# Attention of a decode block in row form: running max with rescaled sums, V in 32 KB rows, c and x as one row

## The chip, the cores and the metric

The kernel runs on one core of a Trainium2 chip. The metric is the device time of one execution in microseconds (us). The runs of the kernel before lie between 439.77 and 440.72 us in all sets (0.2%). A ratio is the mean time of one kernel's fast runs over that of the other's of the same rounds, so it is not quite the ratio of the medians that are quoted.

A note on names: PE is the matmul engine, PEld its weight loads, DVE the vector engine, ACT the scalar engine, POOL the general one, SP the engine that issues the big loads. A packet is the piece of a load that one of the 16 DMA engines moves at a time, here one row of it. All times in the text are on the clock of the profile's views, with 0 at the first instruction; where the recorded texts give the time of a packet, it stands some 0.36 us later than on this clock.

## The reference

One token, one block: a conditioning vector gives six modulation rows, then grouped attention over a cache of 65,536 keys, then a gated feed-forward. Cut to what matters:

```python
# x [1,1,1024]; k_cache, v_cache [1,4,65536,128]; wq [1024,4096]; wo [4096,1024]
mod = silu(c) @ w_mod                       # [1, 6*1024]: sa, ca, ga, sb, cb, gb
h = layernorm(x) * (1 + ca) + sa
q = (h @ wq).reshape(32 heads, 128)         # 8 heads share one K/V head
p = softmax(q @ k.T * 128 ** -0.5)          # over 65,536 keys
x = x + ga * ((p @ v) @ wo)
h = layernorm(x) * (1 + cb) + sb
x = x + gb * ((gelu(h @ w_gate) * (h @ w_up)) @ w_down)
```

Everything is bfloat16. K and V are 64 MB each (67.1 million bytes) and all loads together 185.6 MB, so each byte is used once: a kernel of this kind streams.

## The kernel before

The big loads stand in one list. SP issues them in the order of the list, and each waits until the buffers that it overwrites are free ("released"). Attention runs over 32 chunks of 8,192 keys (2 MB of K, 2 MB of V). A step of PE works on three chunks at once: T (64 transposes of K, 128x128 each) of chunk i, QK of chunk i-1, PV of chunk i-2.

```python
head = iter([8, 0, 2, 4, 6, 8])                         # ten slots of 16 KB a partition
j_mod = [... plan_load(wmod_v[:, k:k + 2, :], ..., next(head), nslot=2) ...]   # 4 loads
j_q   = [... plan_load(wq_v[:, k:k + 4, :], ..., next(head), nslot=2) ...]     # 2 loads
blank = {}                                              # stands for the PV of chunks -2 and -1
for j in (-2, -1):
    blank[j] = Job(None, None, SITES + j % SITES)       # SITES = 4: slots 6 and 7
...
for i in range(NC + 2):                                 # NC = 32 chunks
    if i == SITES:
        j_o = [plan_o(k) for k in range(0, 16, 16)]     # half of wo into slots 8 and 9
    if i < NC and i % KU == 0:                          # KU = 2: K of two chunks, 32 KB rows
        j_k[i] = plan_load(kv_src(kh, i, KU), ..., i % SITES, kfill[...], KU)
    if i >= 2:
        j = i - 2                                       # V of one chunk, 16 KB rows
        j_v[j] = plan_load(kv_src(vh, j), ..., SITES + j % SITES, vfill[j % SITES])
# ... cut: the other half of wo, w_gate, w_up, w_down

def issue_ready():                                      # SP, in the order of the list
    while issued[0] < len(loads):
        j = loads[issued[0]]
        if any(q.freed is None for q in j.prev):
            return
        SP.wait(*(q.freed for q in j.prev))
        sp.dma_start(j.view, j.src).then_inc(j.tok[0], 16)
        issued[0] += 1

# one step of PE; the same instructions serve every four chunks in a hardware loop, so the
# first pass also runs QK of chunk -1 and PV of chunks -2, -1 on whatever is there
def QK(b):          # 64 of these a chunk: K^T (128x128) is the weight, q (8 columns) moves
    pe.matmul(sc_ps[:, base + n * REP:base + (n + 1) * REP], kt_sb[:, j % 2, n, :],
              q_buf[:, j % SITES, :], start=True, stop=True)
def PV(q):          # 64 of these: V (128x128) is the weight, P (8 columns) moves
    pe.matmul(b7[:, s * REP:(s + 1) * REP], j_v[j].view[:, n, :], p_sb[:, s, n, :],
              start=(n == 0), stop=(n == CH - 1))
T(0); QK(0); T(1); QK(1); PV(0); T(2); QK(2); QK(3); PV(1); T(3); PV(2); MT(); PV(3); MB()

for h in range(REP):                                    # ACT: eight exps a chunk
    act.activation(p_sb[:, s, :, h], scv[:, h, :], ACT.Exp, bias=mneg[:, j, h:h + 1],
                   scale=scale, accum_out=z_all[:, j, h:h + 1])
```

Each chunk has its own maximum. After the last chunk all partial sums are rescaled at once.

## Time and profile before

| | before |
|---|---|
| median of the runs | 439.9 us at first, 440.06 us with the runs beside the changed kernel |
| span in the profile | 438.6 us |
| share of the load queue | 98.8% of 16 DMA engines' span |
| PE, DVE, ACT busy | 345.6, 171.9, 146.4 us |
| summed packet time | 434.5 us per DMA engine |

The summary page of the kernel before, cut to the lines used. The span stands first, then the busy time of the engines, then the 40 equal slices of the span (each digit is the busy share in tenths, 9 is 90% or more, and GB/s is what the DMA engines moved), then the load queue with packets, megabytes and its share of 16 engines.

```profile
span 438.6 us, 15324 instructions
...
PE 345.6 (79%) x7107; PEld 315.0 (72%) x7107; DVE 171.9 (39%) x300; ACT 146.4 (33%) x553; POOL 11.7 (3%) x25
...
DMA  8999999999999999999999999999999999999995
GB/s 343 411 442 429 428 432 426 430 432 427 429 435 429 448 420 456 410 445 439 410 451 409 452 409 451 418 433 442 424 434 427 433 430 433 438 434 425 423 424 238
...
q1 hardware_dynamic: 9904, 185.60, 98.8%
...
slots<-in_A_k_cache_dram SPq DMA_DIRECT2D x16, 4096.0 KB, 20.9
slots<-in_A_v_cache_dram SPq DMA_DIRECT2D x32, 2048.0 KB, 26.9
```

The DMA row shows no pause between its first and last slice. PE at 79% looks like a rival. The loads do wait for the buffers that PE frees, but so much is queued meanwhile that the DMA engines do not run dry: a K load needs 9.7 us for its own 4 MB (at 432 GB/s, which is 16 engines with packets of 32 KB at 1214.4 ns each) and lands a median of 20.9 us after its issue, so other loads stand before it.

The second view is the timeline of SP of the kernel before, first lines: start, duration, and the load that was issued. It tells when each load may first move.

```profile
26.19 2.05 SPq L234 DMA_DIRECT2D slots<-in_A_k_cache_dram  x2
36.43 0.80 SPq L234 DMA_DIRECT2D slots<-in_A_v_cache_dram  x2
57.15 0.33 SPq L234 DMA_DIRECT2D slots<-in_A_wo_dram  x1
80.61 0.33 SPq L234 DMA_DIRECT2D slots<-in_A_k_cache_dram  x1
```

The first two V loads go out at 36 us, half of wo at 57 us. When PE begins its first step at 63 us, some 12 MB stand in the queue (K of two more chunks, the first two V loads, half of wo), which is 29 us of transfer. The third view is the chain of waits that ended last, in the stretch where attention begins (start, duration, what):

```profile
26.19 36.92 DMA slots<-in_A_k_cache_dram
63.24 1.89 PE kt_ps L562 x16
65.53 1.73 PE kt_ps L562 x16
```

The first K load lands, and PE's transposes follow.

### The profile page before, as it was taken

What the parts mean: (1) busy time and instruction counts of PE and PEld (TensorE: products, weight loads), DVE (VectorE), ACT (ScalarE), POOL (GpSimd) and SP (SyncE); (2) the same over time, 40 slices, a digit from 0 to 9 for tenths busy, and PEclk for the clock granted to TensorE, in tenths of its full rate; (3) what the DMA queues carried; (4) which work ended last, traced back from release to release, by engine and by line L of the source; (5) the groups of instructions that cost most, each with busy time, mean ns of one, the idle gap of its engine ahead of it and who ended that gap; (6) DMA issues with size and microseconds to landing.
All of it is one profiled execution on the core that took longest, in us unless ns stands there. A gap on an engine that the chain in (4) does not pass through costs nothing.

```text
span 438.6 us, 15324 instructions
## 1 busy us (share of the span) xinstructions
PE 345.6 (79%) x7107; PEld 315.0 (72%) x7107; DVE 171.9 (39%) x300; ACT 146.4 (33%) x553; POOL 11.7 (3%) x25
## 2 busy tenths in 40 slices
PE   0154669997989979998999889999799989547564
PEld 0022348897979979998999779998789989533234
DVE  0101015363644553564445544644445545142100
ACT  1000001434435644343446434345625434600000
POOL 8100000000000000000000000000000000000000
PEclk9995658696977895895579965959858886658955
DMA  8999999999999999999999999999999999999995
GB/s 343 411 442 429 428 432 426 430 432 427 429 435 429 448 420 456 410 445 439 410 451 409 452 409 451 418 433 442 424 434 427 433 430 433 438 434 425 423 424 238
DMA packets 10228, 185.88 MB, mean 424 GB/s; under 512 B 1376, under 2 KB 1376, under 8 KB 1760
## 3 DMA queue, kind: packets, MB, share of 16 engines
q1 hardware_dynamic: 9904, 185.60, 98.8%
q8 instruction: 13, 0.21, 0.2%
q10 hardware_dynamic: 304, 0.01, 0.0%
q14 instruction: 7, 0.06, 0.0%
HBM read 185.60 MB, written 0.00 MB: 423 GB/s over the span
## 4 chain that ended last, share of the span: by engine, by line
DMA 57%; PE 37%; DVE 2%; issue 2%; ACT 1%; SPq 1%; ACTq 0%; POOL 0%
DMA slots<-in_A_v_cache_dram 39%; PE kt_ps L562 18%; DMA slots<-in_A_k_cache_dram 8%; PE b L626 7%; DMA slots<-in_B_w_down_dram 6%; PE sc_ps L582 6%; DMA x_row<-in_A_x_dram 4%; PE kt_ps L393 3%; PE b L606 1%; PE b L373 1%; ACT p_sb L692 1%; PE b L596 1%; SPq L234 1%; DVE kt_sb L752 0%; PE sc_ps L454 0%
## 5 line engine op out<-in xcount | busy, mean ns | idle before, releaser
L562 PE MATMUL kt_ps<-ident,slots 128*128 128x128 bf16 x2048 | 176.7, 256 | 10.2 <-DMA slots<-in_A_k_cache_dram 9.5
L562 PEld LDWEIGHTS kt_ps<-ident,slots 128*128 128x128 bf16 x2048 | 152.6, 117 | 12.0 <-issue 6.6
L661 DVE COPY kt_sb<-kt_ps 128x2048 bf16<-128x2048 bf16 x96 | 117.5, 1224 | 108.9 <-PE kt_ps L562 108.8
L661 ACT ACTIVATE kt_sb<-kt_ps 128x2048 bf16<-128x2048 bf16 x32 | 60.1, 1877 | 178.4 <-PE kt_ps L562 178.4
L626 PE MATMUL b<-p_sb,slots 128*128 128x8 bf16 x2176 | 75.0, 167 | 23.6 <-DMA slots<-in_A_v_cache_dram 11.2
L626 PEld LDWEIGHTS b<-p_sb,slots 128*128 128x128 bf16 x2176 | 68.8, 99 | 26.2 <-issue 12.8
L692 ACT ACTIVATE p_sb<-sc_ps,mneg 128x64 bf16<-128x64 f32 x256 | 83.5, 561 | 7.2 <-DVE mneg L687 7.2
L692 ACT ACTIVATION_READ_ACCUMULATOR p_sb<-sc_ps,mneg 128x1 f32 x256 | 77.1, 366 | 0.0
L582 PE MATMUL sc_ps<-q_buf,kt_sb 128*128 128x8 bf16 x2112 | 69.8, 167 | 1.0 <-issue 1.0
L582 PEld LDWEIGHTS sc_ps<-q_buf,kt_sb 128*128 128x128 bf16 x2112 | 67.8, 100 | 1.1 <-issue 1.1
L393 PE MATMUL kt_ps<-slots,h_pad 128*32 128x512 bf16 x176 | 17.8, 547 | 15.4 <-DMA slots<-in_A_wq_dram 8.3
L393 PEld LDWEIGHTS kt_ps<-slots,h_pad 128*32 128x32 bf16 x176 | 6.1, 124 | 24.8 <-issue 11.2
L680 DVE TENSOR_REDUCE m_col<-sc_ps 128x8 f32<-128x512 f32 x32 | 21.8, 680 | 4.4 <-PE sc_ps L582 4.4
L685 DVE TENSOR_REDUCE mg<-b 8x1 f32<-8x128 f32 x32 | 8.9, 279 | 32.8 <-PE b L596 32.8
L464 PE MATMUL b<-ident,x_row 8*128 8x8 bf16 x1 | 0.2, 161 | 20.2 <-DMA x_row<-in_A_x_dram 20.2
L606 PE MATMUL b<-negi,mg 8*128 8x8 f32 x66 | 14.9, 296 | 0.0
L393 PE MATMUL kt_ps<-slots,s_pad 128*32 128x512 bf16 x96 | 10.7, 516 | 4.9 <-DMA slots<-in_w_mod_dram 4.9
L464 PEld LDWEIGHTS b<-ident,x_row 8*128 8x128 bf16 x1 | 0.1, 97 | 20.1 <-issue 20.1
L687 DVE COPY mneg<-b 128x8 f32<-128x8 f32 x32 | 5.3, 166 | 21.1 <-PE b L606 21.1
L454 PEld LDWEIGHTS sc_ps<-identf,kt_sb 128*128 128x128 f32 (+1 forms) x48 | 7.6, 204 | 8.2 <-DVE kt_sb L775 4.3
L606 PEld LDWEIGHTS b<-negi,mg 8*128 8x128 f32 x66 | 11.9, 223 | 2.2
L454 PE MATMUL sc_ps<-identf,kt_sb 128*128 128x128 f32 (+1 forms) x48 | 9.1, 352 | 4.5 <-DVE kt_sb L775 2.4
(97 smaller groups left out, 89.2 us busy)
## 6 DMA issues: line engine op xcount, KB each, us to landing
slots<-in_A_k_cache_dram SPq DMA_DIRECT2D x16, 4096.0 KB, 20.9
slots<-in_A_v_cache_dram SPq DMA_DIRECT2D x32, 2048.0 KB, 26.9
slots<-in_w_mod_dram SPq DMA_DIRECT2D x4, 3072.0 KB, 20.4
slots<-in_A_wq_dram SPq DMA_DIRECT2D x2, 4096.0 KB, 35.0
slots<-in_A_wo_dram SPq DMA_DIRECT2D x2, 4096.0 KB, 32.5
slots<-in_B_w_gate_dram SPq DMA_DIRECT2D x2, 3584.0 KB, 23.7
slots<-in_B_w_up_dram SPq DMA_DIRECT2D x2, 3584.0 KB, 22.9
slots<-in_B_w_down_dram SPq DMA_DIRECT2D x3, 2048.0 KB, 26.2
```

The costliest lines, as they stand in the source:

```text
L234: sp.dma_start(j.view, j.src).then_inc(j.tok[0], 16)
L393: ins = pe.matmul(out, pad[:, k, :], jb.view[:, kk, c0:c0 + ROW], start=k <= last_k[0], stop=k >= last_k[1], skip_group_check=True,)
L454: ins = pe.transpose(dst[:, i * w:i * w + n], src[:, a], identf[0:src.shape[0], 0:n])
L562: ins = pe.transpose(kt_ps[:, half * 2048 + t * P:half * 2048 + (t + 1) * P], j_k[i - i % KU].view[:, i % KU * CH + b * TB + t, :], ident[ ...
L582: ins = pe.matmul(sc_ps[:, base + n * REP:base + (n + 1) * REP], kt_sb[:, j % 2, n, :], q_buf[:, j % SITES, :], start=True, stop=True,)
L606: ins = pe.matmul(b6[:, 256:256 + REP], mg8[:, j % 2:j % 2 + 1].to_broadcast([REP, P]), negi[:, :], start=True, stop=True,)
L626: ins = pe.matmul(b7[:, s * REP:(s + 1) * REP], j_v[j].view[:, n, :], p_sb[:, s, n, :], start=(n == 0), stop=(n == CH - 1),)
L661: ev[i % SITES][b].done(act.activation(dst, src, ACT.Copy) if E_ is AC else dve.tensor_copy(dst, src))
L680: m1[s].done(dve.tensor_reduce(m_col[:, j % 2, :].unsqueeze(2), scv, AX.X, ALU.max))
L685: m2[s].done(dve.tensor_reduce(mg8[:, j % 2:j % 2 + 1], b6[0:REP, 32:32 + P], AX.X, ALU.max))
L687: v_mc[j] = DVE.done(dve.tensor_copy(mneg[:, j, :], b6[:, 256:256 + REP]))
L692: ins = act.activation(p_sb[:, s, :, h], scv[:, h, :], ACT.Exp, bias=mneg[:, j, h:h + 1], scale=scale, accum_out=z_all[:, j, h:h + 1],)
```

## The change

The intent: PE, busy for 79% of the span, should do the attention with fewer, wider matmuls, ACT should do one wide exp in place of eight narrow ones, V should come in larger pieces, and the small loads of c and x should not be 128 tiny rows. q and P become the stationary operands, in four column tiles of 32, and K^T and V move by 512 columns. P has then to be transposed (PT), which puts PV one step later (LAG = 3). The maximum runs on from chunk to chunk, and DVE rescales the sum of each chunk. The core of the diff, with the epilogue and the constants cut:

```diff
-        act.dma_start(c_in[:, :], c[0].rearrange("(p k) -> p k", p=P)).then_inc(c_sem, 16)
-        act.dma_start(x_in[:, :], A_x[0, 0].rearrange("(p k) -> p k", p=P)).then_inc(x_sem, 16)
-        act.dma_start(x_row[:, :], A_x[0, 0].rearrange("(j p) -> j p", p=P)).then_inc(in_sem, 16)
+        act.dma_start(c_row, c).then_inc(c_sem, 16)
+        act.dma_start(x_row, A_x[0]).then_inc(x_sem, 16)
@@ the list of loads
-        for j in (-2, -1):
-            blank[j] = Job(None, None, SITES + j % SITES)
+        for j in (-2 * VU, -VU):                      # VU = 2
+            blank[j] = Job(None, None, vslot(j))      # slots 4, 5 and slots 6, 7
+            blank[j].freed = None
-        for i in range(NC + 2):
+        for i in range(0, NC + KU, KU):
             if i == SITES:
-                j_o = [plan_o(k) for k in range(0, 16, 16)]
+                j_o.append(plan_o(0, 8))              # a quarter of wo into slot 8
-            if i < NC and i % KU == 0:
+            if i < NC:
                 j_k[i] = plan_load(kv_src(kh, i, KU), flat(KU * CH, DH), i % SITES, ...)
-            if i >= 2:
-                j = i - 2
-                j_v[j] = plan_load(kv_src(vh, j), flat(CH, DH), SITES + j % SITES, ...)
+            else:
+                j_o.append(plan_o(8, 9))
+            if i >= KU:
+                j = i - KU
+                j_v[j] = plan_load(kv_src(vh, j, VU), flat(VU * CH, DH), vslot(j), ..., VU)
@@ QK, per quarter chunk
-                    for t in range(TB):               # 16 of 8 columns
-                        pe.matmul(sc_ps[...], kt_sb[:, j % 2, n, :], q_buf[:, j % SITES, :], ...)
+                    for g in range(NQ):               # 4 of 512 columns, in 4 column tiles
+                        pe.matmul(sc(j)[QD * g:QD * (g + 1), :], q_buf[:, j % SITES, QD * b:QD * (b + 1)],
+                                  kt_sb[:, j % 2, n:n + w, :]..., start=b == 0, stop=b == NB - 1)
@@ PV
-                j = i - 2
+                j = i - LAG
-                        pe.matmul(b7[:, s * REP:(s + 1) * REP], j_v[j].view[:, n, :], p_sb[:, s, n, :], ...)
+                            pe.matmul(b7[QD * c:QD * (c + 1), :]..., p_sb[:, s, c * P + QD * g:...],
+                                      v[:, NQ * g + c, :, :], start=g == 0, stop=g == NQ - 1)
@@ ACT
-                for h in range(REP):
-                    act.activation(p_sb[:, s, :, h], scv[:, h, :], ACT.Exp, ...)
+                act.activation(al[:, j:j + 1], mneg[:, j - 1:j], ACT.Exp, ...)     # the rescale
+                act.activation(p_row[:, j % 2, :], sc(j), ACT.Exp, ..., accum_out=zr[:, j:j + 1])
@@ DVE, per chunk
-                    dve.tensor_copy(o_all[:, j, :], b7[...])
+                    dve.scalar_tensor_tensor(o_acc[:, :], o_acc[:, :], al[:, j:j + 1], b7[:, :], ALU.mult, ALU.add)
```

With LAG = 3 the first pass of the loop runs PV for chunks -3, -2 and -1, and chunk -3 reads slot 5. The first V load (slots 4 and 5) may therefore go out only after PV of PE's first step has run.

## The prediction

> **What bounds the kernel now.** The DMA. The summary page's queue table gives the load queue 98.8% of 16 engines' span, and the slices show 9 (90% or more) between the first and last, 424 GB/s on average. The packet records run from 2 us to 436 us of the 438.6 us span and sum to 434.5 us per engine (no hole). [...] the 32 KB packets here (1214 ns each, 16 engines) make 432[...]. PE is 79% busy, but in the chain of waits its pieces lie between K and V landings: a K load lands a median of 20.9 us after its issue, of which its own 4 MB take about 9.7, so some 11 us of other loads are queued before it.
>
> **What the change does.**
> 1. V in 32 KB instead of 16 KB packets. Mean packet times are 612.7 and 1214.4 ns: 11.1 ns saved per pair, 128 pairs per engine: -1.4 us, fully on the path.
> 2. wo goes from 32 to 16 KB: 16 pairs per engine, +0.2 us.
> 3. c and x as rows: 256 packets of 16 B go (0.14 us per engine), and 16 V completions (0.14 us): -0.3 us. The w_mod matvec starts sooner than 20.8 us, off the path: some 38 us of loads are queued then.
> 4. PE in attention: QK and PV go from 128 matmuls with 128x128 weights (34 to 39 ns each) to 32 of 512 columns in four column tiles (0.107 us each at half clock): about 5 to 3.5 us per chunk. The 64 transposes stay. ACT's eight exps with accumulator reads (2.6 us per chunk) become one wide exp, a rescale and a copy. All off the path: the DMA needs 9.7 us per chunk.
> 5. The softmax end (386.2 to 393 us) becomes a few small matmuls, off the path.
> 6. A new risk: the first V load now waits for the first PE step after K lands (63.2 us), not for w_mod (issued at 36.4 us). That step reaches the end of PV at about 69.5 us (estimated from that step's transposes, 1.9 us per 16), data 1.4 us later, about 71; the loads before it end at 71 to 73 us. I put 0 to 1 us of starved DMA on the path. Later V loads still find about 10 us queued.
>
> **Sum.** 439.9 - 1.4 + 0.2 - 0.3 + 0.4 = 438.8 us. Range 437.4 to 440.4. Chances: faster by over 2% 0.01, within 2% 0.97, slower 0.02.
>
> **What would show each step.** V packets averaging 1214 ns; a summed packet time of about 433 us per engine and a load queue still near 99%. PE busy falling, with its idle time now before K and V landings; ACT busy falling by more than a third. A slice below 9 near 70 us would be the starved start. The chain of waits should still end in w_down's landing and about 3 us after it.
>
> **What would make it wrong.** A larger hole at the first V load; V slots freed in pairs and late, so that the queue runs dry at each pair (GB/s in the slices then falls below 420 throughout); [...] the max chain stretching a chunk beyond 9.7 us; a packet rate that depends on which tensors are in flight.

## The result, and the profile after

| | before | after |
|---|---|---|
| median of 6 runs | 440.06 us (439.77 to 440.30) | 441.28 us (439.90 to 441.69) |
| ratio | | 1.0024, 95% interval 1.0010 to 1.0037 |
| span in the profile | 438.6 us | 439.5 us |
| summed packet time per DMA engine | 434.5 us | 433.0 us |
| mean packet of the load queue, of 16 KB and of 32 KB | 611.7 and 1214.4 ns | 612.0 and 1216.0 ns |
| packets of V | 4096 of 16 KB | 2048 of 32 KB |
| PE, DVE, ACT busy | 345.6, 171.9, 146.4 us | 315.2, 217.3, 111.2 us |

The class was right (within 2%), the sign was not: 438.8 us with a range up to 440.4 was stated, 441.28 us was measured. The same lines of the page, of the changed kernel:

```profile
span 439.5 us, 8993 instructions
...
PE 315.2 (72%) x4077; PEld 208.2 (47%) x4077; DVE 217.3 (49%) x403; ACT 111.2 (25%) x164; POOL 15.7 (4%) x20
...
DMA  8999998999999999999999999999999999999995
GB/s 356 432 441 435 429 428 347 425 429 429 429 429 432 436 435 433 441 435 435 429 429 432 429 432 429 430 435 435 435 441 435 432 415 438 428 436 435 421 420 229
...
q1 hardware_dynamic: 7888, 185.60, 98.3%
...
slots<-in_A_k_cache_dram SPq DMA_DIRECT2D x16, 4096.0 KB, 23.1
slots<-in_A_v_cache_dram SPq DMA_DIRECT2D x16, 4096.0 KB, 23.7
```

PE has 30 us less to do and nothing comes of it, as was expected. The packets cost 1.4 us less in sum over all queues, and 1.1 us less in the load queue (432.2 against 433.3 us per engine). But the seventh slice (65.9 to 76.9 us) moved 347 GB/s, against 426 before; that is the only 8 inside the DMA row. The slice is 11 us long, so its missing fifth is about 2 us.

The timeline of SP of the changed kernel, the same loads:

```profile
26.64 2.05 SPq L236 DMA_DIRECT2D slots<-in_A_k_cache_dram  x2
71.17 0.33 SPq L236 DMA_DIRECT2D slots<-in_A_v_cache_dram  x1
71.54 0.43 SPq L236 DMA_DIRECT2D slots<-in_A_wo_dram  x1
80.92 0.33 SPq L236 DMA_DIRECT2D slots<-in_A_k_cache_dram  x1
```

The first V load goes out at 71.17 us and its bytes move from 72.1 us on, 1.0 us later. Since wo stands after it in the list, wo waits with it, although its slot is free (in a run below, where wo stands earlier, it goes out at 56.17 us). What was issued earlier had drained, but not on all engines at once: in the packet records 16 engines are at work until 70.2 us, four from 70.5 to 71.2 us, one at 72.0 us, and 16 again at 72.9 us. Between 68 and 86 us an engine was idle for 1.7 us on average, against 0.1 us in the kernel before. The chain of waits in this stretch:

```profile
26.64 35.78 DMA slots<-in_A_k_cache_dram
62.42 3.60 issue
66.02 1.88 PE kt_ps L597 x16
68.45 1.49 PE kt_ps L597 x16
```

Here is what the chain of the kernel before did not have: K has landed at 62.42 us and PE begins at 66.02 us. "issue" means that PE waited for nothing that the profile shows.

A second measure is needed to say how much a gap costs. Take the bytes that each kernel has moved by a given moment, from the packet records, and express the lead of one over the other in us at 432 GB/s:

| moment, us | 20 | 60 | 68 | 80 | 150 | 250 | 350 | 420 |
|---|---|---|---|---|---|---|---|---|
| lead of after over before, us | +0.54 | +0.58 | +0.58 | -1.66 | -1.27 | -1.06 | -0.83 | -0.71 |

So the changed kernel wins 0.5 us in its first 20 us, loses 2.2 us between 68 and 80 us, and wins back 0.95 us over all of the attention. Its last load packet ends 1.0 us later than before's (436.4 against 435.4 us), and the times of the two profiled runs differ by as much (440.85 against 439.92 us).

### The profile page after: what moved, and what is told of

Read it like the earlier page. It is cut to its first block, busy times and chain, and to the rows that moved or that the text cites. A ratio compares the mean times of both kernels' runs of the same rounds, so it can differ in the third digit from the quotient of the medians.

```text
span 439.5 us, 8993 instructions
## 1 busy us (share of the span) xinstructions
PE 315.2 (72%) x4077; PEld 208.2 (47%) x4077; DVE 217.3 (49%) x403; ACT 111.2 (25%) x164; POOL 15.7 (4%) x20
## 4 chain that ended last, share of the span: by engine, by line
DMA 54%; PE 32%; DVE 11%; issue 2%; ACT 1%; POOL 0%; DVEq 0%; POOLq 0%
DMA slots<-in_A_k_cache_dram 42%; PE kt_ps L597 15%; DMA slots<-in_B_w_down_dram 8%; PE b L680 5%; PE sc_ps L619 4%; DMA slots<-in_A_v_cache_dram 4%; PE kt_ps L420 3%; DVE selt L353 3%; DVE kt_sb L719 2%; DVE s_pad L759 1%; DVE o_red L742 1%; PE b L646 1%; PE sc_ps L661 1%; DVE o_acc L732 1%; PE b L400 1%
## 5 line engine op out<-in xcount | busy, mean ns | idle before, releaser
L597 PE MATMUL kt_ps<-ident,slots 128*128 128x128 bf16 x2048 | 154.6, 236 | 36.4 <-DMA slots<-in_A_k_cache_dram 27.7
L597 PEld LDWEIGHTS kt_ps<-ident,slots 128*128 128x128 bf16 x2048 | 132.3, 106 | 62.4 <-issue 42.8
L777 ACT ACTIVATE p_sb<-sc_ps 128x512 bf16<-128x512 bf16 x32 | 19.1, 597 | 179.1 <-PE sc_ps L661 179.1
L619 PE MATMUL sc_ps<-kt_sb,q_buf 128*32 128x512 bf16 x528 | 52.1, 429 | 0.0
L680 PE MATMUL b<-slots,p_sb 128*32 128x512 bf16 x560 | 42.0, 426 | 3.2 <-DMA slots<-in_A_v_cache_dram 2.5
L732 DVE SCALAR_TENSOR_TENSOR o_acc<-o_acc,s_pad,b 128x512 f32<-128x512 f32 x28 | 20.9, 748 | 12.1 <-PE b L680 12.1
L680 PEld LDWEIGHTS b<-slots,p_sb 128*32 128x32 bf16 x560 | 16.3, 109 | 19.8 <-issue 8.6
L783 ACT ACTIVATE p_row<-sc_ps,s_pad 128x512 bf16<-128x512 f32 x32 | 21.7, 677 | 0.0
L759 DVE TENSOR_REDUCE s_pad<-sc_ps 128x1 f32<-128x512 f32 x28 | 19.1, 680 | 0.0
L646 PE MATMUL b<-mg,selt 8*128 8x1 f32 x66 | 12.7, 259 | 8.2 <-DVE mg L769 8.2
L646 PEld LDWEIGHTS b<-mg,selt 8*128 8x128 f32 x66 | 9.8, 186 | 11.8 <-DVE mg L769 11.7
L463 POOL TENSOR_TENSOR rs<-va,halfneg 128x1 f32<-128x1 f32 x2 | 1.1, 554 | 379.8 <-DVE va L460 379.8
```

Of the source, the lines that this page charges most:

```text
L597: ins = pe.transpose(kt_ps[:, half * 2048 + t * P:half * 2048 + (t + 1) * P], j_k[i - i % KU].view[:, i % KU * CH + b * TB + t, :], ident[ ...
L619: ins = pe.matmul(sc(j)[QD * g:QD * (g + 1), :], q_buf[:, j % SITES, QD * b:QD * (b + 1)], kt_sb[:, j % 2, n:n + w, :].rearrange("p n d -> ...
L646: ins = pe.matmul(b6[:, 256:257], selt[:, :], mg[:, j % 2:j % 2 + 1], start=True, stop=True,)
L680: ins = pe.matmul(b7[QD * c:QD * (c + 1), :].rearrange("p (b d) -> p b d", b=NB), p_sb[:, s, c * P + QD * g:c * P + QD * (g + 1)], v[:, NQ ...
L732: v = oc[j % SITES].done(dve.scalar_tensor_tensor(o_acc[:, :], o_acc[:, :], al[:, j:j + 1], b7[:, :], ALU.mult, ALU.add))
L759: v = DVE.done(dve.tensor_reduce(m_new, sc(j), AX.X, ALU.max))
```

## The experiments

Two theories. **H (the hole):** all of the loss is the one gap at 70 us, made by the order of the load list and the first PE step; the rest of the change is a small gain. **S (steady state):** V slots freed in pairs and a step late, or the new PE step, cost time all along. From the chain came a third question, **F**: why PE began 3.6 us after K had landed. The instruction queue's packet records ("q8 instruction" of the page, 10 packets of 16 KB in the changed kernel) show a packet of 16 KB at 63.42 us, 0.95 us long, and no other start in that queue between 29.8 and 69.1 us. F is the author's reading of that packet, to be tested: what PE runs after the wait for K came in this packet (a "block" in the texts below), and it was fetched only once that wait had passed.

All kernels below gave correct results. The kernel before ran beside them at 440.04 us in both sets. In four of them (wo_first, late, wo_first_late, before_v32) the runs fall into two groups 2 to 3 us apart, whose granted clocks do not differ, and in the first three the profiled run lies in the upper group. What parts the groups is open.

### wo_first: w_o ahead of the first V load

Edit, on the changed kernel:

```diff
-            if i == SITES:
-                j_o.append(plan_o(0, 8))
             if i < NC:
                 j_k[i] = plan_load(...)
-            else:
-                j_o.append(plan_o(8, 9))
+            if i == KU:
+                j_o += [plan_o(0, 8), plan_o(8, 9)]
             if i >= KU:
                 j_v[i - KU] = plan_load(...)
```

> The changed kernel with one edit: the two w_o loads into slots 8 and 9 (4 MB together, about 9.7 us of transfer) stand before the first V load in the load queue instead of after it and at the end. Theory H (hole): after lost 2.2 us at 70 to 76 us because the first V load waits for PE's first step; with 9.7 us of other bytes queued the gap closes, no 2 us stretch between 66 and 80 us falls below 90% of the mean rate, and the time is 441.3 - 2.2 = 439.1 us (438.3 to 439.7), below the kernel before (440.06). Rival S (steady state: V slots freed in pairs and a step late, or PE's new step, cost the time all along): the gap at 70 us may close but the time stays within 0.5 us of 441.3.

Measured: 439.27 us (six runs, five from 438.99 to 439.53, one of 441.57), ratio to before 0.9979 (0.9966 to 0.9992). The timeline of SP:

```profile
56.17 0.80 SPq L236 DMA_DIRECT2D slots<-in_A_wo_dram  x2
71.17 0.33 SPq L236 DMA_DIRECT2D slots<-in_A_v_cache_dram  x1
```

V still goes out at 71.17 us, but the lead over before stays at +0.5 us from 68 to 80 us: the gap is closed, and 2.0 us of the time go with it. S is out as the main cause, since PE and the V slots are as they were.

The profiled run was the one of 441.57 us, and it shows a gap of its own. The stretches of 360 to 370 us of this kernel (length, busy time of PE, PEld, DVE, ACT and POOL with counts, granted clock, DMA share, GB/s; a packet counts where it started, so that a share can pass 1):

```profile
360.00:365.00 5.00, 4.33 (x68) 3.42 (x64) 3.33 (x8) 2.71 (x4) 0.00 (x0) 1.00 0.95 341
365.00:370.00 5.00, 5.00 (x82) 3.35 (x81) 4.64 (x6) 1.08 (x3) 0.00 (x0) 1.00 0.97 413
```

The edit had also taken the second w_o load away from its place before the last V pair, so that the queue ran thin there: the lead over before falls by 1.25 us between 360 and 380 us. The other five runs are 2 us faster; whether they had this gap is not known.

### late, and wo_first_late: the loop held back, without and with w_o first

Edit of both, on the changed kernel and on wo_first:

```diff
+        GP.wait(v_q)
+        GP.wait(GP.done(pool.memset(kt_sb[:, 1, 0:48, :], 0.0)))
+        v_late = GP.done(pool.memset(kt_sb[:, 1, 16:64, :], 0.0))
-        PE.wait(t1, v_const, v_q, v_zero)
+        PE.wait(t1, v_const, v_q, v_zero, v_late)
```

> The changed kernel with PE's loop held back: two clears of an unused tile on POOL (about 5.2 us each) after q is ready, which PE waits for, so that PE's first step starts at 69.4 us (or at 72.8 if the 3.6 us stall seen before it is repeated) instead of 66.0. Theory H: the first V load goes out that much later and every us is lost: time up by the shift of PE's first instruction, 3.2 to 6.8 us, so 444.5 to 448 us. Rival S: PE has slack, the queue catches up, and the time rises by less than half of the shift.

Measured, late: 447.93 us (446.45, 446.62, 449.24, 449.63). The chain of waits of this kernel:

```profile
65.25 5.23 POOL kt_sb L790
70.47 3.70 issue
74.17 1.89 PE kt_ps L597 x16
```

POOL ended at 70.47 us and PE began at 74.17 us: the stall of 3.7 us is there again. The first V load went out at 79.85 us, 8.7 us later than in the changed kernel, and the profiled run took 449.63 us, 8.8 us more than the profiled run of the changed kernel (440.85). In this run every us of the delay is lost, and it is not made up in the 350 us that follow: the lead over before is -10.2 us at 90 us and -9.4 us at 420 us, a gain of 0.8 that the changed kernel has as well (-1.6 to -0.7). In the stretches of late the DMA rests, while PE, when it starts, works:

```profile
70.00:76.00 6.00, 1.82 (x19) 1.63 (x19) 0.00 (x0) 0.00 (x0) 0.47 (x1) 0.50 0.05 16
76.00:86.00 10.00, 9.80 (x137) 6.84 (x140) 5.26 (x5) 1.88 (x1) 0.00 (x0) 0.86 0.54 210
```

> Both edits: w_o's two loads first, and PE's loop held back as in the run before. Theory H: the first V bytes come at 76 to 79 us, the queue holds bytes until about 80 us, so the delay costs nothing: within 0.6 us of the kernel with w_o first alone (about 439.1), although PE starts 3 to 7 us later. Rival S: the same rise as in the run with the delay alone.

Measured, wo_first_late: 443.23 us (442.00 to 444.83), 4.0 us above wo_first by the medians (2.8 us between the two profiled runs, since that of wo_first has its second gap as well). The number stated (within 0.6 us) was missed, because PE began not at 72.8 us or earlier but at 76.99 us: POOL ended near 70.7 us, and the instruction packet came only at 74.39 us. V went out at 82.86 us, and its first bytes moved at 83.8 us; the engines began to run dry at 80.2 us. The lead over before falls by 3.9 us between 80 and 90 us, and that is the 4 us that were lost. So a filler of 9.7 us turned a delay of 11.7 us in the first V load into a loss of 4.0, which is H's arithmetic with a longer delay than planned, and not the same rise as without the filler, as S would have it.

### shift: PE's instructions moved

Edit, on the changed kernel:

```diff
         v_xp = PE.done(ins)
+        for _ in range(64):           # at 7 us, PE idle; overwritten later
+            pe.matmul(kt_fp[0:1, 0:1], ident[0:1, 0:1], ident[0:1, 0:1], start=True, stop=True)
```

> The changed kernel with 64 one-element matmuls on PE at about 7 us, where PE has nothing to do (their result is overwritten): PE's program up to its attention loop is 128 instructions longer. Theory F (fetch): PE started its first step 3.6 us after the first K load had landed (62.4 us) because the instructions after that wait lay in a block that was fetched only then (a 16 KB instruction packet at 63.8 us); with the block limits moved, PE starts within 1.5 us of the landing (62.4 to 64 us), the first V load goes out at 67.5 to 69 us instead of 71.2, the 2.2 us gap closes to under 0.6 us and the time falls by 1.6 to 2.2 us, to about 439.4. Rival: PE waits for something else (q, the clears on POOL, K's last bytes): PE still starts at 66 us and the time stays at 441.3.

Measured: 440.13 us (439.18, 439.18, 440.13, 440.34, 440.38). The timeline of PE in this kernel (the bracket gives the idle time before it and what ended it):

```profile
62.89 1.88 PE L600 MATMUL kt_ps<-ident,slots 128*128 128x128 bf16 x16 [3.38 <-DMA slots<-in_A_k_cache_dram]
```

PE begins when K lands, at 62.89 us, with nothing but unrelated instructions put 55 us earlier: this is what F says, and q, the clears and K's bytes are excluded as the cause. The instruction packets of this kernel come at 47.6 and 65.6 us, none in the stall's place. The kernels with the stall say the same. The records do not name the engine that an instruction packet is for, but in all six of these kernels (wo_one and wo_one_v16 stand below) PE began 1.6 to 1.7 us after a 16 KB instruction packet had ended, though these packets started anywhere from 63.36 us (wo_one_v16) to 74.39 us (wo_first_late). Two things stay open. A wait for q and the set-up stands just before PE's loop, and the wait for K inside it; which of them held the packet back is not shown. Nor is it shown whether the late packet alone does it, or the entry into PE's loop, which lies there too. The timeline of SP:

```profile
69.17 0.33 SPq L237 DMA_DIRECT2D slots<-in_A_v_cache_dram  x1
```

The first V load goes out close to the 69.5 us of the prediction. That is 2.0 us earlier than in the changed kernel and not 3.1, because the first step now lies more in a time of half clock (PE's granted clock was 0.5 until 68.7 us here, for 5.8 of the 6.3 us from PE's start to the V load, and until 69.4 us in the changed kernel, for 3.4 of 5.2 us; 16 transposes took 1.88 us at a granted clock of 0.5 and 1.07 us at 1.0). The loss between 68 and 80 us falls from 2.2 to 0.5 us. The median falls by 1.15 us, less than the 1.6 expected; the profiled run is one of the two of 439.18 us, and the gap of the three slower ones was not seen.

### wo_one, and wo_one_shift: the smallest cure, and both

Edit of wo_one, on the changed kernel (wo_one_shift has the 64 matmuls as well):

```diff
-            if i == SITES:
-                j_o.append(plan_o(0, 8))
             if i < NC:
                 j_k[i] = plan_load(...)
             else:
                 j_o.append(plan_o(8, 9))
+            if i == KU:
+                j_o.append(plan_o(0, 8))
```

> As with both w_o loads first, but only one of them (2 MB, 4.9 us) stands before the first V load; the other keeps its place before the last V pair. Theory: the gap at 70 us is closed (first V bytes at 72.5 us, queue until about 75), and the second gap that moving both had opened at 361 to 368 us (1.2 us lost in its profile) is gone too, so the profile has no gap over 0.3 us, and the time is 438.6 us (438.0 to 439.3), 1.4 below the kernel before. Rival: what remains of the packet gain is not there and the time equals that of the kernel before within 0.4 us.

Measured, wo_one: 439.30 us (439.07 to 439.46), ratio to before 0.9984 (0.9970 to 0.9998). The stretches of 70 to 76 us of before, of the changed kernel and of wo_one, one fence each, columns as above:

```profile
70.00:76.00 6.00, 5.18 (x131) 5.05 (x128) 2.85 (x3) 1.88 (x1) 0.00 (x0) 1.00 0.92 391
```

```profile
70.00:76.00 6.00, 5.80 (x91) 3.98 (x84) 3.04 (x3) 1.88 (x1) 0.00 (x0) 1.00 0.74 279
```

```profile
70.00:76.00 6.00, 6.00 (x89) 4.46 (x87) 2.77 (x3) 0.73 (x1) 0.00 (x0) 0.92 1.01 426
```

279 GB/s against 426: the gap is gone. The runs are also much closer together than those of the changed kernel. But 438.6 us were stated, and the gain on before is 0.74 us, not 1.4.

> One w_o load first and the 64 one-element matmuls: both cures of the same gap. Theory H: the gap is closed by either, so together they give no more than 0.3 us over one w_o load first (about 438.6), though PE starts 2 to 3.6 us sooner; it may vary less from run to run. Rival: PE's start matters in itself, and the time falls by another 1 us or more.

Measured, wo_one_shift: 439.20 us (439.13 to 439.35), ratio 0.9982 (0.9969 to 0.9996). PE begins at 63.03 us in this kernel and at 67.17 us in wo_one, and the times differ by 0.1 us. In this kernel PE's start matters only for the load that waits for it.

### before_v32, and wo_one_v16: the packets of V alone

before_v32 is the kernel before with V in pairs; its attention, its c and x loads and its early first V load stay.

```diff
+VU = 2
-            if i >= 2:
+            if i >= 2 and i % VU == 0:
                 j = i - 2
-                j_v[j] = plan_load(kv_src(vh, j), flat(CH, DH), SITES + j % SITES, vfill[j % SITES])
+                j_v[j] = plan_load(kv_src(vh, j, VU), flat(VU * CH, DH), SITES + j % SITES, vfill[...], VU)
@@ PV: view[:, j % VU * CH + n, :]; the pair is released after its second chunk
```

> The kernel before with one part of the change alone: V in 16 loads of 4 MB (32 KB packets) instead of 32 of 2 MB; the attention and the c, x loads as before, so the first V load goes out at 36 us as before. The packet term: -1.4 us for packets and -0.1 us for 16 fewer completions: 440.06 - 1.5 = 438.5 us (438.0 to 439.3), ratio about 0.9966, with V packets of about 1214 ns. Rival S (pairs free V slots late): no gain or a loss, 440 us or more.

Measured: 439.29, 439.53, 439.60, 439.86, 442.12 and 442.57 us; ratio with all six 1.0013 (0.9989 to 1.0037), unclear. The four lower runs are 0.5 us below before, not 1.5. What the two others met is open: none of them was profiled. In the profiled run (439.53) w_gate goes out at 379.8 us, 6.5 us later than in the kernel before, since PE reaches the end of its transposes only after the last pairs of V; a gap there is conceivable and was not seen.

wo_one_v16 is wo_one with each V load issued as two halves of 16 KB rows:

```diff
+            if j.half:
+                sp.dma_start(j.view[:, 0:CH, :], j.src[:, 0:CH, :]).then_inc(j.tok[0], 16)
+                sp.dma_start(j.view[:, CH:, :], j.src[:, CH:, :]).then_inc(j.tok[0], 16)
+            else:
                 sp.dma_start(j.view, j.src).then_inc(j.tok[0], 16)
@@ V's semaphore counts 32 a pair
```

> One w_o load first, and each 4 MB load of V as two loads of 2 MB (16 KB packets) issued together: the packet size alone. By the prediction's term the time rises by 1.4 us for packets and 0.14 for completions against one w_o load first; by the bytes moved in the traces (after gained 0.9 us on before between 100 and 420 us) it rises by 0.9 to 1.1. If the packet size is worth nothing, the two are equal.

Measured: 439.97 us (439.83 to 440.06), 0.67 us above wo_one, in runs of one set whose ranges do not touch. So the packet size is worth 0.67 us, about two thirds of the packet time that it saves (in the two traces the load queue's packets sum to 431.85 and 432.89 us per engine, 1.04 us apart). Where the rest goes is not shown. One candidate is the end of the stream: the time ends with the slowest of 16 engines, and they do not end together. At 434.0 us, 8 of 16 are still moving bytes in before, and 2 in wo_one. wo_one is 1.2 us ahead of before in bytes at 420 us, but its last packet ends only 0.8 us earlier (434.6 against 435.4 us). What makes the last engines late was not tested.

wo_one_v16 has all of the change except the large packets and the hole, and it takes the time of the kernel before: 439.97 against 440.04 us, ratio 0.9999 (0.9985 to 1.0012). The new attention and the rows of c and x are worth nothing that these runs can see.

## Why the prediction was right or wrong

- **"What bounds the kernel now. The DMA."** Right. PE lost 30 us of work and ACT 35 us, and no run shows a us of it in the time. In wo_one and wo_one_shift PE's start differs by 4 us and the time by 0.1.
- **Step 1, V in 32 KB packets, -1.4 us "fully on the path".** There is a gain, of half the size: V's packets are worth 0.67 us of time (wo_one against wo_one_v16). Part of the miss is in the input. The 612.7 ns is the mean of all 16 KB packets of the kernel before, 13 instruction packets of 928 ns among them; the 4096 of V alone took 611.7 ns, which makes 9.0 ns a pair and -1.15 us. The other part is that packet time was booked one to one as time: between wo_one_v16 and wo_one the packets of an engine got 1.04 us shorter in sum, and the kernel 0.67 us faster.
- **Step 2, w_o in 16 KB packets, +0.2 us.** Not measured by itself; the packet means above make it +0.14 us.
- **Step 3, c and x as rows, -0.3 us.** Right in kind: the changed kernel leads by 0.54 us at 20 us, where before_v32, with the old c and x loads, leads by 0.08. No gain in time is shown, though: wo_one_v16 has the same lead of 0.56 us at 20 us and ends with the kernel before. The w_mod matvec did not start sooner: 20.98 us, against 20.78. It waited, off the path, for DVE, whose set-up stood until 15.43 us, while clears on POOL ran until 15.36 us (last section), and whose next work began at 19.3 us.
- **Steps 4 and 5, PE, ACT and the softmax end off the path.** Right for the time. "ACT busy falling by more than a third" was wrong: it fell by a quarter, 146.4 to 111.2 us. DVE rose by 45 us, 12 of them the set-up operation that stood.
- **Step 6, "I put 0 to 1 us of starved DMA on the path". This is the step that failed.** It was carried into the sum as +0.4 us; the runs show 2.2 us by bytes and 2.0 us by time (441.28 against 439.30 in wo_one). The place, the load and the reason were right: the first V load waits for PE's first step. The term was mis-sized at both ends of the gap. Its end: PE was taken to begin when K lands. It began 3.6 us later, after a 16 KB instruction packet (63.42 us, 0.95 us long) had come, and the first V load went out at 71.17 us instead of 69.5, its bytes at 72.1 instead of 71. Its beginning: "the loads before it end at 71 to 73 us" is right for the last engine (72.1 us) but not for the others, 12 of which ran out of bytes between 70.2 and 70.5 us. When the stall is removed (shift), V goes out at 69.17 us and the bytes lost are 0.5 us, inside what was stated; so the stall is the larger part.
- **The sum.** Stated: -1.1 us. Measured: +1.2 us, of which +2.0 for the hole and -0.74 for all the rest (wo_one against before). The hole was too small by 1.6 us and the gains too large by 0.8; the gains alone would have left the time in the range.
- **"What would make it wrong": "A larger hole at the first V load".** That is what happened. V slots freed late, the second item, did not: the GB/s row stays between 415 and 441 from the eighth slice to the thirty-ninth.

The versions wo_one and wo_one_shift are faster than both kernels, by 0.16 and 0.18% against before, with intervals that exclude 1.

## What to carry to other kernels

When a kernel is bound by its loads, look for the one load that a change makes wait for a compute step, and count the bytes queued before it to the us: here a delay cost nothing until they had drained on the first engines (PE began 4.1 us later in wo_one than in wo_one_shift, for 0.1 us of time), and after that all of itself (late: V 8.7 us later, 8.8 us of time), and it was not won back. Loads in one list wait in order, so a load whose buffer is free belongs ahead of one that waits; here moving one line was worth 2 us. And the first instruction after a long wait can come late, here by 3.3 to 6.3 us in six kernels: leave a margin of several us there.

## Measured here and left open

- The first instruction after a long wait: PE began 3.6 us (changed kernel), 4.7 us (wo_one) and 3.7 us (late) after what it waited for, each time with a 16 KB packet of the instruction queue in between, which ended 1.6 to 1.7 us before PE began; with 64 matmuls and their weight loads put ahead in PE's program (shift) it began at once (62.89 us). While the load queue moved 377 to 459 GB/s the packet itself came as late as 3.7 us after the wait (wo_first_late, 70.67 to 74.39 us), and while it moved 16 GB/s 1.1 us (late, 70.47 to 71.61 us). The runs do not show whether the entry into PE's loop has a part in these delays.
- The size of a row: a load packet of 16 KB took 611.7 ns and one of 32 KB 1214.4 ns in the kernel before, and V in the larger ones was worth 0.67 us of 440.
- The 16 engines of one stream end apart. In the kernel before, 8 of 16 still worked at 434.0 us, and the last ended at 435.4; in the changed kernel 12 of 16 ran out of bytes between 70.2 and 70.5 us, and the last of the other four at 72.1 us.
- DVE beside clears on POOL: in the changed kernel a DVE operation on 8x128 elements took 12.31 us (3.12 to 15.43 us, and the one behind it 12.18 us, to the same moment), while POOL ran a row of six clears from 2.26 to 15.36 us. No run left the clears out, so it is not shown that they held it.
